# One written order for the change from the first to the second MLP, on all queues of one core

## The chip, the core and the metric

The kernel runs on one core of one Trainium2 chip. The metric is the device time of one execution in microseconds; before the change the median of three runs is 956.58 us (955.93 to 958.93). A core has five queues that work side by side: TensorE (PE, matmuls), VectorE (DVE), ScalarE (ACT), GpSimd (POOL) and SyncE (SP, which issues the transfers). Each of them takes its own instructions in one order, fixed when the program is built, and an instruction starts when the semaphores that it names have been reached.

## The reference

Sliding-window attention with a linear bias, and on its output two MLPs one after the other, both with a squared ReLU; the first has a scale s and an offset b. There are 2304 tokens (4 batches of 576), a model width of 512 and a hidden width of 2048, all in float32.

```python
attn_out = _attn_ref(q, k, v)                                # (4, 8, 576, 64)
x = attn_out.transpose(0, 2, 1, 3).reshape(2304, 512)
h = x @ moe_w_in;  r = np.maximum(h, 0.0)
x = (s * (r * r) + b) @ moe_w_out                            # first MLP
h = np.maximum(x @ moe2_w_in, 0.0)
out = (h * h @ moe2_w_out).astype(np.float32)                # second MLP
```

## The kernel before

Every float32 matmul of the MLPs is made of three matmuls on halves: a value is split into a rounded high part and the rest, and high times high, high times low and low times high are summed. The weights arrive as 64-bit words and are turned into such halves on the chip.

**Steps.** An MLP goes block by block over the tokens: four blocks of 512 tokens (the first MLP takes the first of them as two of 256) and a tail block of 256 that gathers the last 64 tokens of each batch. A block has 16 steps, one per 128 hidden columns. A step (`step_of`, L410) has a first layer of 12 matmuls into one PSUM bank (`first`, L414), a squaring (`square`, L428: ACT takes the ReLU out of the bank, DVE multiplies and frees the bank), a halving (`halves`, L437: ACT rounds to the high part, DVE subtracts), and a second layer of 12 matmuls (`one_second`, L451) that adds to the block's output banks. The first layers use two banks in turn, so the first layer of step n+2 waits until DVE has squared step n. All wide steps (512 tokens) share the one buffer `r_all`, so ACT's ReLU of a step waits for the halving of the step before. `mlp` (L474) writes the steps one after the other, with the second layers up to two steps behind the first.

**Names.** The change from the first to the second MLP has 37 steps, numbered 0 to 36: 16 narrow ones of the tail block of the first MLP (banks `ha`, 256 columns), five wide ones that are left of that MLP's last full block (`ha`, 512 columns; steps 4, 5, 10, 11, 12), and from step 21 on the 16 of block 0 of the second MLP (`hb`). `ga` and `gb` are the halved squares, `oa` and `ob` the output banks, `xoa` the outputs on their way to memory.

**What runs beside them.** In this stretch the second MLP's weights are loaded and converted, in 32 parts of 512 KB (4 groups of 8: four of `w_in`, four of `w_out`). A part is loaded into one of three staging buffers `st`, goes through a first stage (ACT, DVE), a second (ACT, DVE, two on POOL) and a third (ACT writes the high part `wih` or `woh`, DVE the low part `wil` or `wol`), which frees the buffer for the load of the third part after it. Group g of the second MLP takes the place of group g of the first, so the first of its third stages waits until the last step that reads the old group is done. Also in this stretch: the outputs of the two blocks of the first MLP are copied out of PSUM and written, the column sum for the offset is made (`pc`, `bcol`), and the second MLP's inputs `xib` are read back (`fetch`, L649), scaled by s with the offset added (four instructions on ACT per 256 tokens) and halved into `y` (`place`, L658: one DVE cast and one DVE subtraction per 256 tokens).

**What sets the order.** PE keeps the written order in the whole kernel. The attention stage is pinned: a table `START` (L39) lists its pieces, and the wrapper `InOrder` (L19) ties each instruction of ACT, DVE, POOL and SP to the one written before it, as long as `pinned` holds `True`. At L627 `pinned` is cleared. From there on a scheduler orders these four queues by its own estimates; `at(n, ...)` (L611) says before or after which step a piece is written, and `turns` (L693) hands out one conversion after the other, all three stages and the next load in one piece.

Of the kernel before, what the change touches and what calls it, by code (L numbers as in the profile page):

```python
# [50 lines left out]
"""  # L51

UNIT_ENGINES = """svvvvs vvvvss vvsvss vvvvsv vvvvvs vvvvss vvvvsv vsvssv vvvvss vvvvsv vvvvss vvvvss vvvvss vvsvsv vsvssv ssvsvv""".split()


@with_exitstack
def attention_mlp2_kernel(ctx, tc, first0, first1, qkv0, qkv1, qkvt, w_in1, w_out1, s_in, b_in, w_in2, w_out2, out):
# [76 lines left out]
    def act_copy(o, i):  # L134
        return scalar.activation(o, i, AF.Copy)
# [31 lines left out]
    def group_loads(g, wts, w_in, w_out, staging, steps):  # L167

        f0 = g * GF * P
        parts = [(w, k, n, st) for k, w, st in ((0, w_in, steps[0]), (2, w_out, steps[1])) for n in range(0, GF, st)]
        places = {}

        def load(i):
            if i == 0:
                wts.append({})
            w, k, n, step = parts[i]  # L180
            rows, n = slice(f0 + n * P, f0 + (n + step) * P), step
            if k == 0:
                w, rows, n = w[:, 2 * rows.start:2 * rows.stop], slice(None), NCC
            src = w[rows].rearrange("(a p) n -> p a n", p=P)
            t = places[i] = staging(i, f"st{g}{i}").rearrange("p a n -> p (a n)").rearrange("p (a n) -> p a n", a=n)

            with tc.issue_after(last_load[0]) if last_load else nullcontext():
                wdma.append(sync.dma_start(t, src).ins)

        def stages(i):  # L190
            def third():
                _, k, n, step = parts[i]
                if k not in wts[g]:
                    for j in (k, k + 1):
# [212 lines left out]
    def job(nm, x, wts, second, width, finish, o_tags, h_tags):  # L407
        return dict(nm=nm, x=x, wts=wts, second=second, width=width, finish=finish, o_tags=o_tags, h_tags=h_tags, po=[], n=0)
# [42 lines left out]
    def one_second():  # L451

        d, f, gh, lo, w, start, stop, _ = todo.pop(0)
        if start:
            d["po"] += [psum(d["o_tags"](), f"o{d['nm']}{i}") for i in range(d["width"] // P)]
        d["second"](d["po"], d["wts"][f // GF], f % GF, gh, start, stop, lo, w)
        if stop:
            d["finish"](d["po"])

    def second_layer(room):  # L460

# [54 lines left out]
    def finish1(nm, dram):  # L516
        def f(po):
            for t in range(2):
                xo = result(f"xo{nm}{t}")
                act_copy(xo, po[t])  # L520
                sync.dma_start(dram[:, 2 * t:2 * t + 2, :].rearrange("p a n -> p (a n)"), xo)
        return f

    def finish_pair(nm, i):
        def f(po):
            for o in range(NCC):
                xo = result(f"xo{nm}{o}", o > 1)
                (act_copy, vector.tensor_copy)[o % 2](xo, po[o])
                for u in range(2):
                    sync.dma_start(acc_dram[i + u][:, o, :], xo[:, u * BLK:(u + 1) * BLK])  # L530
        return f

    def finish2(nm, b):
        def f(po):
            for t in range(len(po)):
                ob = result(f"ob{nm}{t}", b == order[-1] and t > 0)
                if b == order[-1] and t == len(po) - 1:
                    for y, copy in enumerate((act_copy, vector.tensor_copy)):
                        cols = slice(y * BLK, (y + 1) * BLK)
                        copy(ob[:, cols], po[t][:, cols])  # L540
                        sync.dma_start(out[b * S + t * P:b * S + (t + 1) * P, cols], ob[:, cols])
                    continue
                (act_copy, vector.tensor_copy)[t % 2](ob, po[t])
                if b == "tail":
                    for r in range(P // TAIL):
                        row = (t * (P // TAIL) + r) * S + 2 * BLK
                        sync.dma_start(out[row:row + TAIL, :], ob[r * TAIL:(r + 1) * TAIL, :])
                else:
                    row = b * S + t * P
                    sync.dma_start(out[row:row + P, :], ob)  # L550
        return f

    blocks = [(b, u) for b in range(B) for u in range(2)] + ["tail"]
# [13 lines left out]
    def run(pieces):  # L567
        for p in pieces:
            p()
# [41 lines left out]
    def at(n, *pieces):  # L611
        slots.setdefault(n, []).extend(pieces)
# [36 lines left out]
    def fetch(nm, dram):  # L649

        xi = bp.tile([P, NCC, BLK], F32, tag="xi", name=f"xi{nm}")
        with tc.issue_after(last_load[0]) if last_load else nullcontext():
            sync.dma_start(xi, dram)
        for o in range(NCC):
            scalar.activation(xi[:, o, :], xi[:, o, :], AF.Identity, bias=bcol[:, o:o + 1], scale=s_sb)
        return xi

    def place(nm, xis):  # L658
        t = new_pair(nm)
        for u, xi in enumerate(xis):  # L660
            c = slice(u * BLK, (u + 1) * BLK)
            split(t[0][:, :, c], t[1][:, :, c], xi, vector.tensor_copy, dve_sub)
        return [y[:, :, :len(xis) * BLK] for y in t]
# [16 lines left out]
    def in_bp(i, nm):  # L680
        return bp.tile([P, 1, 2 * DM], I32, tag="st", name=nm, bufs=3)

    h_tags, y0, slots = tags("h", "t"), [], {}
    p6["h_tags"] = h_tags
    t8 = job(f"a{LAST}", lambda: x_tail[0], wts1, second_t, BLK, finish1(f"a{LAST}", acc_dram[LAST]), tags("s"), h_tags)
# [4 lines left out]
    groups = [group_loads(g, wts2, w_in2, w_out2, in_bp, (1, 1)) for g in range(NG)]  # L690
    loads, convs = [sum((x[k] for x in groups), []) for k in range(2)]
# [10 lines left out]
    cur = y0[2]  # L702
    last_load.clear()
    order = [0, 1, 2, "tail", 3]
    o_tags = tags("o", "o", "va", "vb", "s", "s")
    for b, after in zip(order, order[1:] + [None]):
        if b:
            last_load[:] = [wdma[-1]]
# [55 lines left out]
```

## Time and profile before

| | us |
|---|---|
| median of three runs | 956.58 (955.93 to 958.93) |
| the profiled execution, its own time | 956.87 |
| its span, first to last instruction | 955.1 |
| the 37 steps and one more: first matmul of step 0 to first matmul of block 1's second step | 464.88 to 645.11 |

The profile is of one execution. Its first part gives the busy time of each engine: PE is busy for 97% of the span. A busy share says little on a queue that waits for others in places, so the rows below are cut by stretches of time. "Idle before" in a row of the timeline is the time that the engine stood idle just before that instruction, and behind the arrow stands what ended it. Matmuls overlap: a row's duration (0.39 us at 512 columns) is longer than the distance to the next one's start. The clock is TensorE's granted clock as a share of the full 2.4 GHz; the other level is 1.2 GHz.

### The profile page before, as it was taken

The page shows a single profiled execution, that of the slowest core. Times are in us where ns is not written, and L with a number is a line of the kernel's source. Part 1 is how long each engine was busy: PE and PEld are TensorE (multiplying, and loading weights), DVE is VectorE, ACT ScalarE, POOL GpSimd, SP SyncE. Part 2 cuts the span into 40 slices and gives each one's busy share as a digit, 9 for nine tenths or more (in the row PEclk, how much of TensorE's full clock was granted, in tenths as well). Part 3 has the DMA queues.
Part 4 walks back from the last instruction along what each step waited for, and adds up shares of the span by engine and source line. Part 5 has one row for each costly group of instructions (what it writes and reads, how often), then busy time and mean ns, then how long its engine had stood idle before and what let it go on. Part 6 is the DMA issues. An engine that isn't in the chain of part 4 may idle for free.

```text
span 955.1 us, 13902 instructions
## 1 busy us (share of the span) xinstructions
PE 925.0 (97%) x5256; PEld 772.4 (81%) x5256; DVE 485.5 (51%) x1178; ACT 448.1 (47%) x1010; POOL 102.2 (11%) x164
## 2 busy tenths in 40 slices
PE   6899999999999999999999998999999999999998
PEld 4789998787777787777788886788888888998886
DVE  7988776445454455454377767444223222422222
ACT  7988775434444344454566666344223222422222
POOL 4333220000000000000124333100000000000000
PEclk7999999999999999999999999999999999999999
DMA  8642532201121111310334544012001000100001
GB/s 308 217 137 98 169 106 73 66 23 39 34 70 36 45 45 30 104 45 1 110 133 149 172 143 135 20 45 89 1 1 48 19 1 1 45 1 23 1 1 44
DMA packets 44227, 67.49 MB, mean 71 GB/s; under 512 B 6016, under 2 KB 27776, under 8 KB 44160
## 3 DMA queue, kind: packets, MB, share of 16 engines
q1 hardware_dynamic: 44160, 66.60, 21.6%
q8 instruction: 41, 0.67, 0.3%
q14 instruction: 26, 0.21, 0.1%
HBM read 57.15 MB, written 9.44 MB: 70 GB/s over the span
## 4 chain that ended last, share of the span: by engine, by line
PE 81%; DMA 6%; ACT 6%; DVE 5%; issue 1%; POOL 1%; SPq 0%; ACTq 0%; DVEq 0%
PE ha L29 18%; PE oa L29 17%; PE ob L29 16%; PE hb L29 16%; PE s L29 6%; DMA st<-w_out 3%; PE hbtail L29 2%; ACT st L29 2%; PE obtail L29 2%; DMA st<-w_in 2%; DVE st L29 2%; PE u L29 2%; PE s_t L29 1%; DVE wil L29 1%; PE u_t L29 1%
## 5 line engine op out<-in xcount | busy, mean ns | idle before, releaser
L29 DVE SCALAR_TENSOR_TENSOR r_all<-hb,r_all 128x512 f32<-128x512 f32 x64 | 44.1, 690 | 160.5 <-ACT r_all L29 160.2
L29 ACT ACTIVATE r_all<-hb 128x512 f32<-128x512 f32 x64 | 38.1, 595 | 171.1 <-PE hb L29 170.3
L29 POOL TENSOR_TENSOR st<-st 128x256 int32<-128x256 int32 x128 | 94.0, 761 | 210.8 <-DVE st L29 197.0
L29 DVE SCALAR_TENSOR_TENSOR r_all<-ha,r_all 128x256 f32<-128x256 f32 (+1 forms) x96 | 52.8, 553 | 102.1 <-ACT r_all L29 101.9
L29 ACT ACTIVATE st<-st 128x512 int32<-128x512 uint32 (+3 forms) x100 | 79.2, 813 | 29.6 <-DMA st<-w_in 12.0
L29 ACT ACTIVATE r_all<-ha 128x256 f32<-128x256 f32 (+1 forms) x96 | 46.2, 484 | 93.7 <-PE ha L29 92.2
L29 PE MATMUL oa<-ga,woh 128*128 128x256 f32 x384 | 73.1, 289 | 0.1
L29 PEld LDWEIGHTS oa<-ga,woh 128*128 128x128 f32 x384 | 60.7, 193 | 4.9 <-issue 3.5
L29 ACT ACTIVATE pr<-pr,nd 128x256 f32<-128x256 f32 (+1 forms) x102 | 48.0, 475 | 29.7 <-DVE nd L29 27.6
L29 DVE SCALAR_TENSOR_TENSOR st<-st 128x512 int32<-128x512 int32 (+1 forms) x50 | 44.1, 885 | 26.0 <-ACT st L29 22.9
L29 PE MATMUL oa<-ga,wol 128*128 128x256 f32 x192 | 54.4, 283 | 0.0
L29 PE MATMUL ha<-x0h,wih 128*128 128x256 f32 x128 | 37.3, 292 | 0.0
L29 PE MATMUL ha<-x0h,wil 128*128 128x256 f32 x128 | 36.4, 284 | 0.6 <-DVE wil L29 0.6
L29 PEld LDWEIGHTS oa<-ga,wol 128*128 128x128 f32 x192 | 36.9, 192 | 0.0
L29 PE MATMUL ha<-x0l,wih 128*128 128x256 f32 x128 | 36.2, 283 | 0.0
L29 PE MATMUL s<-raw 64*128 64x256 f32 (+1 forms) x224 | 32.5, 391 | 3.3 <-issue 1.5
L29 DVE CUSTOM_DVE_ANT_0 pr<-s,bases 128x256 f32<-128x256 f32 (+1 forms) x96 | 32.3, 386 | 3.5 <-PE s L29 3.4
L375 POOL MEMSET pr_t<- 128x64 f32 x16 | 2.4, 151 | 289.8 <-PE s L29 227.4
L29 DVE TENSOR_SCALAR st<-st 128x512 int32<-128x512 int32 (+1 forms) x50 | 28.2, 565 | 4.8 <-ACT st L29 3.4
L29 PE MATMUL hb<-y0h,wih 128*128 128x512 f32 x64 | 25.5, 398 | 5.2 <-DVE r_all L29 5.2
L29 PE MATMUL ha<-x3h,wih 128*128 128x512 f32 x64 | 27.1, 423 | 2.3 <-DVE r_all L29 2.3
L29 PEld LDWEIGHTS s<-raw 64*128 64x128 f32 x224 | 19.3, 191 | 9.7 <-issue 4.3
(685 smaller groups left out, 2599.0 us busy)
## 6 DMA issues: line engine op xcount, KB each, us to landing
st<-w_out SPq DMA_DIRECT2D x20, 512.0 KB, 4.4
st<-w_in SPq DMA_DIRECT2D x8, 1024.0 KB, 6.8
st<-w_in SPq DMA_DIRECT2D x16, 512.0 KB, 4.4
st<-w_out SPq DMA_DIRECT2D x6, 1024.0 KB, 8.1
raw<-qkv SPq DMA_DIRECT2D x36, 128.0 KB, 3.0
xib<-acc SPq DMA_DIRECT2D x9, 512.0 KB, 3.8
raw<-qkv SPq DMA_DIRECT2D x24, 160.0 KB, 3.0
out<-obb SPq DMA_DIRECT2D x15, 256.0 KB, 2.9
```

The lines of the kernel that those rows point to most:

```text
L29: ins = op(*args, **kw)
L375: nc.gpsimd.memset(pr[:, :Z], 0.0)
```

## The change

A second table, `HANDOVER`, lists the pieces of the 37 steps and of all that runs beside them in one order, and `pinned` is set for this stretch, so that ACT, DVE, POOL and SP keep that order instead of the scheduler's. The letters stand for: L, G, H, M the first layer, squaring, halving and second layer of a step (M always takes the oldest that is left); l, a, b, c with group and part the load and the three stages of a conversion; Y the load of 256 tokens of input; F and Q the scaling and halving of one half of them; E and W the copy out of PSUM and the write of an output; B the column sum. Inputs are handled in halves of two column groups, on ACT (s) or DVE (v) as two lists of letters say; the outputs' copies too. The input of block 1 is fetched, scaled and halved within the table. Output buffers `raw` are four instead of three, and the outputs no longer use the staging buffers, but for the last one of the kernel. Each of the pieces is written as before otherwise; PE has the same number of instructions, in a different order.

```diff
+HANDOVER = """
+    L0 G0 H0 L1 l00 l01 L2 G1 L3 a00 b00 B M c00 M0 l04 l02 a04 H1 a01 M1 G2 b01 G3 H2 L4 b04 H3 M2 M3 c01 L5 l05
+    a02 G4 b02 H4 c04 a05 l03 Y0 G5 c02 l06 a03 b05 H5 L6 G6 H6 c05 Y1 M4 l07 L7 a06 M5 G7 M6 b03 H7 b06 a07 F01
...
+EVICT_ENGINES, INPUT_ENGINES = "vsvs ss".split(), "vss svs svs svv vvs vvv vss vss".split()
...
-            return pools["bp"].tile([P, DM], F32, tag="raw", name=nm, bufs=3)
+            return pools["bp"].tile([P, DM], F32, tag="raw", name=nm, bufs=4)
...
+    def ways_out(nm, po, o, places, engine):
+        made = []
+        def evict():
+            made.append(result(f"xo{nm}{o}"))
+            copy_on[engine](made[0], po[o])
+        def write():
+            n = DM // len(places)
+            for u, (dram, c) in enumerate(places):
+                sync.dma_start(dram[:, c, :].rearrange("p a n -> p (a n)"), made[0][:, u * n:(u + 1) * n])
+        return evict, write
...
-                ob = result(f"ob{nm}{t}", b == order[-1] and t > 0)
+                ob = result(f"ob{nm}{t}", b == order[-1] and t > 2)
...
+    def scaled(xi, o, engine="s"):
+        if engine == "s":
             scalar.activation(xi[:, o, :], xi[:, o, :], AF.Identity, bias=bcol[:, o:o + 1], scale=s_sb)
+        else:
+            vector.tensor_scalar(xi[:, o, :], xi[:, o, :], s_sb, bcol[:, o:o + 1], ALU.mult, ALU.add)
...
+    def halve_input(u, h, engine):
+        if u // 2 not in ys:
+            ys[u // 2] = new_pair(f"y{u // 2}")
+        hi, lo = [y[:, 2 * h:2 * h + 2, u % 2 * BLK:(u % 2 + 1) * BLK] for y in ys[u // 2]]
+        split(hi, lo, xis[u][:, 2 * h:2 * h + 2, :], copy_on[engine], dve_sub)
...
-    run(loads[:3])
-    turns = [[*a, b] for a, b in zip(convs, loads[3:] + [lambda: None] * 3)]
-    for n in (4, 4, 5, 5, 6, 7, 8, 9, 10, 10, 11, 11, 12, 12, 13, 14, 15, 17, 18, 19):
-        at(2 * n, *turns.pop(0))
-    at(4, sum_column)
-    at(16, lambda: y0.append(fetch_y(0)))
-    at(24, lambda: y0.append(fetch_y(1)))
-    at(32, lambda: y0.append(place("y0", y0[:2])))
-    mlp(pieces_of(steps), slots)
...
+    pieces = pieces_of(steps + [(b0, f, 0, 2 * BLK) for f in range(NF)])
...
+    pinned.append(True)
+    run(table[x] for x in HANDOVER.split())
+    pinned.clear()
+    cur = ys[1]
+    for b, after in zip(order[1:], order[2:] + [None]):
...
-            at(26 if b == 0 else 2, lambda: nxt.append(load_y(after)))
-        for n in range(NF if b == 0 else 0):
-            if turns and n:
-                at(2 * n, *turns.pop(0))
+            at(2, lambda: nxt.append(load_y(after)))
```

**ACT at the start of the stretch.** Here `r_all<-ha_2` is the ReLU of step 2, on which PE waits for its bank; `xib` is the scaling of an input.

Before:

```order
L29 ACTIVATE r_all<-ha_1_4668 128x256
L29 ACTIVATE st_4648<-st_4648 128x512
L29 ACTIVATE st_4646<-st_4646 128x512
L29 ACTIVATE ga_1_4683<-r_all 128x256
L29 ACTIVATE st_4648<-st_4648 128x512
L29 ACTIVATE xib_4962<-xib_4962,bcol,s_sb 128x256 x4
L29 ACTIVATE xib_5164<-xib_5164,bcol,s_sb 128x256 x4
L29 ACTIVATE r_all<-ha_2_4704 128x256
L29 ACTIVATE wih_4760<-st_4644 128x4x128
```

Now:

```order
L29 ACTIVATE r_all<-ha_1_4662 128x256
L29 ACTIVATE st_4675<-st_4675 128x512 x2
L29 ACTIVATE wih_4731<-st_4675 128x4x128
L29 ACTIVATE st_4749<-st_4749 128x512
L29 ACTIVATE ga_1_4755<-r_all 128x256
L29 ACTIVATE st_4677<-st_4677 128x512
L29 ACTIVATE r_all<-ha_2_4679 128x256
```

The eight scalings stood between steps 1 and 2; now none stands there, and the first of them follows behind step 7.

**DVE at the halving of step 12.** `ga_12l` is the low half that step 12's second layer reads; `y0h` and `y0l` are the halves of block 0's input.

Before:

```order
L29 CAST y0h<-xib_4962 128x4x256
L29 CAST y0h<-xib_5164 128x4x256
L29 TENSOR_SCALAR st_5046<-st_5046 128x512
L29 SCALAR_TENSOR_TENSOR r_all<-ha_12_5170,r_all 128x512
L29 TENSOR_TENSOR y0l<-xib_4962,y0h 128x4x256
L29 TENSOR_SCALAR st_5099<-st_5099 128x512
L29 TENSOR_TENSOR y0l<-xib_5164,y0h 128x4x256
L29 SCALAR_TENSOR_TENSOR st_5109<-st_5109 128x512
L29 TENSOR_TENSOR ga_12l<-r_all,ga_12h 128x512
```

Now:

```order
L29 TENSOR_TENSOR ga_11l<-r_all,ga_11h 128x512
L29 TENSOR_SCALAR st_5040<-st_5040 128x512
L29 TENSOR_SCALAR st_5077<-st_5077 128x512
L29 SCALAR_TENSOR_TENSOR r_all<-ha_12_5136,r_all 128x512
L29 TENSOR_TENSOR ga_12l<-r_all,ga_12h 128x512
L29 TENSOR_TENSOR wil_5111<-st_5040,wih_5110 128x4x128
```

Four instructions that stood between the squaring and the halving of step 12 are gone from there; the halves of `y0` now come from step 15 on, in pieces.

**ACT at the halving of step 5.** `ga_5h` is its high half; `woh<-st` and `wih<-st` are third stages of conversions.

Before:

```order
L29 ACTIVATE r_all<-ha_5_4839 128x512
L29 ACTIVATE wih_4760<-st_4764 128x4x128
L29 ACTIVATE ga_5h<-r_all 128x512
L29 ACTIVATE woh_4876<-st_4774 128x512
L29 ACTIVATE r_all<-ha_6_4882 128x256
```

Now:

```order
L29 ACTIVATE woh_4856<-st_4749 128x512
L29 ACTIVATE st_4842<-st_4842 128x512
L29 ACTIVATE r_all<-ha_5_4829 128x512
L29 ACTIVATE wih_4731<-st_4751 128x4x128
L29 ACTIVATE st_4862<-st_4862 128x512
L29 ACTIVATE st_4842<-st_4842 128x512
L29 ACTIVATE ga_5h<-r_all 128x512
L29 ACTIVATE r_all<-ha_6_4882 128x256
```

The first stage of part 3 of group 0 (`st_4862`), which waits for a load, and a second stage now stand between the ReLU and the halving of step 5.

## Rows read from the trace of the kernel before

**Rows 1.** The page, busy us (share of the span) x instructions.

```profile
PE 925.0 (97%) x5256; PEld 772.4 (81%) x5256; DVE 485.5 (51%) x1178; ACT 448.1 (47%) x1010; POOL 102.2 (11%) x164
```

**Rows 2.** Windows: stretch, width, busy us (instructions) by engine, clock, DMA share, GB/s.

```profile
465.00:485.00 20.00, 18.00 (x116) 16.47 (x115) 10.86 (x22) 14.69 (x30) 4.46 (x6) 0.91 0.53 192
485.00:520.00 35.00, 34.72 (x211) 30.97 (x210) 25.55 (x43) 23.48 (x44) 13.61 (x18) 1.00 0.44 136
520.00:535.00 15.00, 11.84 (x66) 10.20 (x65) 12.98 (x21) 8.72 (x18) 6.85 (x8) 0.89 0.58 182
535.00:605.00 70.00, 64.83 (x346) 55.02 (x346) 48.18 (x78) 43.42 (x78) 25.43 (x33) 1.00 0.40 127
605.00:645.00 40.00, 40.00 (x178) 33.14 (x177) 15.72 (x23) 14.73 (x27) 0.00 (x0) 1.00 0.08 27
```

**Rows 3.** Waits of PE, 470 to 660 us: total us, times, longest.

```profile
PE hb L29 <- DVE r_all L29: 5.2, 4, 3.6
PE oa L29 <- DVE ga_12l L29: 3.2, 1, 3.2
PE ha L29 <- DVE r_all L29: 2.3, 2, 2.0
```

**Rows 4.** Timeline of PE: start, us, operation, [idle before <-what ended it].

```profile
464.88 0.28 PE L29 MATMUL ha<-xtailh,wih 128*128 128x256 f32 x1
...
467.75 0.40 PE L29 MATMUL oa<-ga_74h,woh 128*128 128x512 f32 x1
...
471.32 0.36 PE L29 MATMUL ha<-xtailh,wih 128*128 128x256 f32 x1
...
634.23 0.39 PE L29 MATMUL hb<-y0h,wih 128*128 128x512 f32 x1
...
636.95 0.39 PE L29 MATMUL ob<-woh,gb_13h 128*128 128x512 f32 x1
...
645.11 0.39 PE L29 MATMUL hb<-y1h,wih 128*128 128x512 f32 x1
```

**Rows 5.** Timeline of ACT at step 2.

```profile
473.04 4.05 ACT L29 ACTIVATE xib<-xib,bcol,s_sb 128x256 f32<-128x256 f32 x8 [0.86 <-DVE bcol L29]
477.00 0.36 ACT L29 ACTIVATE r_all<-ha 128x256 f32<-128x256 f32 x1
```

**Rows 6.** Timeline of DVE at the halving of step 12.

```profile
521.78 1.26 DVE L29 TENSOR_TENSOR y0l<-xib,y0h 128x1024 fp32r<-128x1024 f32 x1
...
523.72 1.21 DVE L29 TENSOR_TENSOR y0l<-xib,y0h 128x1024 fp32r<-128x1024 f32 x1
...
525.87 1.10 DVE L29 TENSOR_TENSOR ga_12l<-r_all,ga_12h 128x512 fp32r<-128x512 f32 x1
```

**Rows 7.** Timeline of ACT at step 25, the fifth of block 0.

```profile
579.18 1.22 ACT L29 ACTIVATE st<-st 128x512 int32<-128x512 uint32 x2 [2.10 <-DMA st<-w_in]
580.60 1.26 ACT L29 ACTIVATE st<-st 128x512 f32<-128x512 f32 x2 [0.20 <-DVE st L29]
581.74 0.58 ACT L29 ACTIVATE r_all<-hb 128x512 f32<-128x512 f32 x1
```

**Rows 8.** The staging tiles `st`, 460 to 620 us: durations min/median/max, and loads to landing.

```profile
L29 POOL TENSOR_TENSOR st<-st x64: 607/722/1596, 469.1 to 602.6; 128x256 int32<-128x256 int32 x64
L29 DVE TENSOR_TENSOR wol<-st,woh x16: 677/693/1097, 491.3 to 604.4; 128x512 fp32r<-128x512 f32 x16
DMA to landing us min/median/max: 3.3/4.4/5.6
```

**Rows 9.** Waits of ACT for loads, 464 to 605 us: total us, times, longest.

```profile
ACT st L29 <- DMA st<-w_in: 12.0, 10, 2.5
ACT st L29 <- DMA st<-w_out: 11.7, 13, 2.0
```

**Rows 10.** Groups by line and shape, 464 to 605 us: busy us, mean ns, idle before.

```profile
L29 ACT ACTIVATE st<-st 128x512 int32<-128x512 uint32 x32 | 21.6, 676 | 23.8 <-DMA st<-w_in 12.0 <-DMA st<-w_out 11.7
L29 DVE TENSOR_SCALAR st<-st 128x512 int32<-128x512 int32 x32 | 15.8, 492 | 3.0 <-ACT st L29 2.0
```

**Rows 11.** Timeline of DVE at the halving of step 5.

```profile
490.30 1.10 DVE L29 TENSOR_TENSOR ga_5l<-r_all,ga_5h 128x512 fp32r<-128x512 f32 x1
```

More of the change, by code (lines that the diff above doesn't have):

```diff
@@ L457, in one_second @@
         if stop:
-            d["finish"](d["po"])
+            for p in d["finish"](d["po"]):
+                p()
     def second_layer(room):
@@ L512, in result, with finish1, finish_pair @@
         if "bp" in pools:
-            return pools["bp"].tile([P, DM], F32, tag="raw", name=nm, bufs=3)
+            return pools["bp"].tile([P, DM], F32, tag="raw", name=nm, bufs=4)
         return ap.tile([P, DM], F32, tag="pr", name=nm, bufs=NPR)
-    def finish1(nm, dram):
+    copy_on = {"s": act_copy, "v": vector.tensor_copy}
+    def finish1(nm, dram, engines="ss"):
         def f(po):
[L518 to L521, printed above, removed]
+            evict, write = zip(*(ways_out(nm, po, t, [(dram, slice(2 * t, 2 * t + 2))], engines[t]) for t in range(2)))
+            return evict + write
         return f
-    def finish_pair(nm, i):
+    def finish_pair(nm, i, engines="svsv"):
         def f(po):
[L526 to L530, printed above, removed]
-        return f
+            return sum((ways_out(nm, po, o, [(acc_dram[i + u], slice(o, o + 1)) for u in range(2)], engines[o]) for o in range(NCC)), ())
+        return f
+    def ways_out(nm, po, o, places, engine):
[8 more added lines that the diff above has]
+        return evict, write
     def finish2(nm, b):
@@ L550, in f @@
                     sync.dma_start(out[row:row + P, :], ob)
+            return ()
         return f
@@ L653, in fetch @@
             sync.dma_start(xi, dram)
-        for o in range(NCC):
+        return xi
+    def scaled(xi, o, engine="s"):
+        if engine == "s":
             scalar.activation(xi[:, o, :], xi[:, o, :], AF.Identity, bias=bcol[:, o:o + 1], scale=s_sb)
-        return xi
+        else:
+            vector.tensor_scalar(xi[:, o, :], xi[:, o, :], s_sb, bcol[:, o:o + 1], ALU.mult, ALU.add)
     def place(nm, xis):
@@ L660, in place @@
         for u, xi in enumerate(xis):
+            for o in range(NCC):
+                scaled(xi, o)
             c = slice(u * BLK, (u + 1) * BLK)
@@ L681, in in_bp, with ends, f, load_input @@
         return bp.tile([P, 1, 2 * DM], I32, tag="st", name=nm, bufs=3)
-    h_tags, y0, slots = tags("h", "t"), [], {}
+    h_tags = tags("h", "t")
     p6["h_tags"] = h_tags
-    t8 = job(f"a{LAST}", lambda: x_tail[0], wts1, second_t, BLK, finish1(f"a{LAST}", acc_dram[LAST]), tags("s"), h_tags)
+    t8 = job(f"a{LAST}", lambda: x_tail[0], wts1, second_t, BLK, None, tags("s"), h_tags)
+    ways = {6: finish_pair("a6", 6, EVICT_ENGINES[0]), 8: finish1("a8", acc_dram[8], EVICT_ENGINES[1])}
+    out_of = {}
+    def ends(i):
+        def f(po):
+            out_of[i] = ways[i](po)
+            return ()
+        return f
+    p6["finish"], t8["finish"] = ends(6), ends(8)
+    order = [0, 1, 2, "tail", 3]
+    o_tags = tags("o", "o", "va", "vb", "s", "s")
+    ys, xis = {}, {}
+    def load_input(u):
+        xis[u] = fetch(f"b{u}", acc_dram[u])
+    def scale_input(u, h, engines):
+        for z in range(2):
+            scaled(xis[u], 2 * h + z, engines[z])
+    def halve_input(u, h, engine):
[3 more added lines that the diff above has]
+        split(hi, lo, xis[u][:, 2 * h:2 * h + 2, :], copy_on[engine], dve_sub)
+    b0 = job("b0", lambda: ys[0], wts2, second_n, 2 * BLK, finish2("b0", 0), o_tags, h_tags)
     steps = []
@@ L689, in attention_mlp2_kernel @@
         steps += [(p6, f, 0, 2 * BLK) for f in ((11, 12), (13, 14, 15), (), ())[g]]
-    groups = [group_loads(g, wts2, w_in2, w_out2, in_bp, (1, 1)) for g in range(NG)]
-    loads, convs = [sum((x[k] for x in groups), []) for k in range(2)]
-    run(loads[:3])
-    turns = [[*a, b] for a, b in zip(convs, loads[3:] + [lambda: None] * 3)]
-    for n in (4, 4, 5, 5, 6, 7, 8, 9, 10, 10, 11, 11, 12, 12, 13, 14, 15, 17, 18, 19):
-        at(2 * n, *turns.pop(0))
-    at(4, sum_column)
-    at(16, lambda: y0.append(fetch_y(0)))
-    at(24, lambda: y0.append(fetch_y(1)))
-    at(32, lambda: y0.append(place("y0", y0[:2])))
-    mlp(pieces_of(steps), slots)
[L702 to L708, printed above, removed]
+    pieces = pieces_of(steps + [(b0, f, 0, 2 * BLK) for f in range(NF)])
+    table = {"M": one_second, "B": sum_column}
+    for g in range(NG):
+        for i, (l, c) in enumerate(zip(*group_loads(g, wts2, w_in2, w_out2, in_bp, (1, 1)))):
+            table.update({f"{x}{g}{i}": p for x, p in zip("labc", [l] + c)})
+    for n, piece in enumerate(pieces):
+        table.update({f"{x}{n}": p for x, p in zip("LGHM", piece)})
+    for i, n in ((6, NCC), (8, 2)):
+        for o in range(n):
+            x, y = (2 * o, 2 * o + 1) if i == 6 else (o, o + 2)
+            table.update({f"E{i}{o}": lambda i=i, x=x: out_of[i][x](), f"W{i}{o}": lambda i=i, y=y: out_of[i][y]()})
+    for u in range(4):
+        table[f"Y{u}"] = lambda u=u: load_input(u)
+        for h in range(2):
+            e = INPUT_ENGINES[2 * u + h]
+            table[f"F{u}{h}"] = lambda u=u, h=h, e=e: scale_input(u, h, e[:2])
+            table[f"Q{u}{h}"] = lambda u=u, h=h, e=e: halve_input(u, h, e[2])
+    pinned.append(True)
[3 more added lines that the diff above has]
+    for b, after in zip(order[1:], order[2:] + [None]):
+        last_load[:] = [wdma[-1]]
         nxt, slots = [], {}
```

10 lines of the change are left out of this document (added).

## The prediction

> **What bounds the kernel now.** I read the page's busy shares first: PE is busy for 925.0 of 955.1 us, DVE for 485.5, ACT for 448.1 [rows 1]. PE sets the time, and a change can give back only what PE loses. Its work is the same after the change (as many matmuls, in another order), so the question is how much PE loses in the 37 steps, and how much of that a new order can remove.
>
> Cut by stretches, PE lacks 2.00 us in 465 to 485, 0.28 in 485 to 520, 3.16 in 520 to 535 and 5.17 in 535 to 605, together 10.6 us; from 605 on it is full [rows 2]. The waits put nearly all of it down to DVE: 5.2 us on the squaring in block 0, 3.2 us on the low half of step 12, 2.3 us on the squaring in the narrow and wide steps of the first MLP [rows 3]. The clock is lost twice beside that: 0.91 over the 20 us around the wait at step 4 and 0.89 over the 15 us around the one at step 12, so in both places the lower level, 1.2 GHz, was granted for part of the time [rows 2]; 20 x 0.09 + 15 x 0.11 = 3.5 us. The 5.17 us of 535 to 605 cost no clock (1.00).
>
> What PE would need without any loss: a narrow layer takes (467.75 - 464.88) / 2 = 1.435 us, a wide one 636.95 - 634.23 = 2.72 us, and the second layer of the last step before together with the column sum 471.32 - 467.75 = 3.57 us [rows 4]. From 464.88 to the start of block 1's second step there are 32 narrow layers (45.9 us), that pair (3.57) and 42 wide layers (114.2): 163.7 us. The ten wide layers of the first MLP in this stretch run a little slower (some 0.03 us each), so 164.0. The trace takes 645.11 - 464.88 = 180.2 us [rows 4]. **The loss is 16.2 us**: 10.6 idle, 3.5 of clock, and the remaining 2 at the restarts, where the first matmul after a wait is slow and the idle time counts only from the modelled end of the last one.
>
> **The three large waits, and what the change does to each.** The first: ACT scales both inputs of block 0 in one run of eight, 473.04 to 477.09, and only then takes the ReLU of step 2, at 477.00 [rows 5]; PE waits 2.0 us for the bank and then runs at a lower clock. In the new order the eight scalings are gone from there, and between the ReLUs of steps 1 and 2 stand five stages of conversions and one halving. Counted from the end of step 1's first layer these take 6 x 0.6 = 3.6 us on ACT (two stages in 1.22 us [rows 7]), 2 to 3 us in which the third stage waits for DVE and POOL, and the squaring, some 7.5 us. PE has 9.3 us of other layers between the same two points (two narrow first layers, the column sum, one wide and two narrow second layers), so this wait goes. The second: between the squaring and the halving of step 12 stand two subtractions for `y0` (1.26 and 1.21 us) and two instructions of conversions, so that `ga_12l` comes at 525.87 [rows 6]; now it follows the squaring at once, and PE asks for it one wide second and three narrow first layers, 7.0 us, after step 12's first layer, some 4 us after it is ready. The third: in block 0's fifth step ACT does two first stages, waiting 2.10 us for a load, and two second stages before the ReLU, which comes at 581.74 [rows 7]; in the new order one first stage stands between the ReLUs of the fourth and the fifth step, and PE asks for the bank only three wide layers (8.2 us) after the fifth step's first layer. These three are 2.0 + 3.2 + 3.6 us of idle time and all of the clock. The remaining 1.9 us are four waits of under 0.8 us on the squaring; the new order puts the ReLU in front of the conversions there too.
>
> **What the moved work needs.** The conversions are all still there. Over 465 to 605 DVE is busy for 10.9 + 25.6 + 13.0 + 48.2 = 97.6 us and ACT for 90.3 [rows 2], of 140; the new order spreads them, and the input of block 1 as well, over 156 us (steps 0 to 36 at 164.0 less three wide layers), up to the last steps of block 0. Ten of the sixteen scalings of blocks 0 and 1 go to DVE. Such a scaling on DVE is in no row; on ACT one takes 0.5 us [rows 5], and a DVE instruction with constants over twice the columns takes 0.49 [rows 10]. Between 0.2 and 0.6 us each, I take the 0.49, 5 us in all; with the last steps of block 0 and block 1's input, which the old trace has in 605 to 645 (15.7 us on DVE [rows 2]), DVE stands at 118 of 156 us. If it were full there, each further us would be one of PE; it isn't by some 38.
>
> The staging buffers set the pace of the conversions: a load takes 4.4 us to land (3.3 to 5.6) [rows 8], the three stages some 4 to 5 us more, so three buffers allow one part in about 3 us, or 97 us for 32 parts. There are 150 for them. Only at the start are the margins small, because the third stages of group 0 wait for steps 0 to 3.
>
> **Where the new order can make PE wait.** I went along the new order from one first layer to the next, adding durations behind whatever ends last. Two places have no margin.
>
> Step 5's halving: the third stage of `w_out`'s first part waits until step 3's second layer is done, as the old group is read until then. Counted from there: third stage on ACT and DVE 1.35 us, the load into the buffer that this frees 4.4, its first stage on ACT 0.68, the second stage of another part 0.6, the high half of step 5 0.6, and behind it on DVE `ga_5l` 0.69: 8.3 us. PE in that time does one wide and one narrow first layer, a wide second and a narrow first: 2.72 + 1.44 + 2.72 + 1.44 = 8.3. With a load of 5.6 us it is 1.2 us late, with one of 3.3 early by as much. In the trace before, `ga_5l` took 1.10 us [rows 11] instead of some 0.69, as do some other DVE subtractions (677 to 1097 ns), while POOL's adds take 607 to 1596 [rows 8]; I take 0.4 for that and 0.2 for the hand-overs, so 0.6 us of waiting.
>
> The Trainium skill speaks against placing a halving there: its page "SBUF — State Buffer", section "Who interferes with whom", has a DVE instruction with two SBUF inputs and a GpSimd one that reads SBUF lock each other out for a whole instruction. The slowed rows agree that DVE loses time, but with 0.41 us, less than POOL's median of 0.72. By the page's rule the wait at step 5 would be 0.9 us and the time 0.3 us longer.
>
> Step 10's halving is the same case: the load behind the third stage of `w_in`'s last part, then its first stage, then `ga_10h`. Counted from the end of step 9's first layer: a halving, a scaling and the ReLU on ACT 1.5, the third stage 1.35, the load 4.4, the first stage 0.68, `ga_10h` 0.6, `ga_10l` 0.69, together 9.2 us; PE has three narrow and two wide layers, 9.8. That is a margin of 0.6 us, and 0.6 late if the load takes 5.6. Step 11 has as much. I take 0.5 us for the two together.
>
> From step 16 on every margin that I find is over 1 us, and growing: ACT and DVE go ahead of PE there, since nothing but the ReLU of the next step holds them.
>
> **Edits at nothing.** Outputs copied by another engine, in four own buffers: six copies, each hidden by the 38 us that DVE has, due only when block 0 or block 1 takes the bank. SP's order: all writes but the last wait for a copy made over 5 us earlier, so no load of weights is held by one. The kernel's last outputs in other buffers: the same copies, at most one load's wait of 4 us if a buffer were still being read, which it is not one block later. Block 1's input within the table: done before step 34, needed after step 36.
>
> **Sum.** 956.87 of the profiled execution - 16.2 + 0.6 + 0.5 = 941.6; the median of the runs is 0.3 lower than that execution. I say 941.8.
>
> **The rivals.**
> *New waits with a lower clock.* The old places are gone, but two others stall as long as the first and the second did: 2.0 + 1.8 + 0.3 and 3.2 + 1.7 + 0.3 = 9.3 us. For it: two places without margin, and an order of 32 chained loads in which a late one holds the next. Against: PE waits 0.28 to 0.76 us in the old trace four times without losing any clock. 956.9 - 16.2 + 9.3 = 950.0.
> *The waits only move.* The order was not the cause, the loads were: the same 10.6 us of idle time return elsewhere, with clock and restarts. For it: ACT waited 23.7 us for loads [rows 9]. Against: at the two waits with clock loss no load stands in the chain [rows 5, 6]. 956.9.
> *Slower: a load in front of everything.* In the fixed order each first stage on ACT stands ahead of ReLUs, and a late load holds them all. ACT waited 23 times, 1.03 us on average [rows 9], mostly with nothing to do behind it; if PE pays each, 956.9 - 16.2 + 23.7 = 964.4. It is slower than before from 16.2 / 32 = 0.5 us per part. Against: from step 21 on most loads land before ACT comes to their stage.
>
> **Chances.** The forecast 0.71, its own range 940.4 to 944.5 (all loads early, or step 5, 10 and 11 at the late end with one short loss of clock); two new waits 0.17; moved 0.06; slower 0.06. The range of 8 in 10 is 940.0 to 951.0. A measurement of this kernel can tell 0.3% (2.9 us) from no change: faster by that 0.88, same 0.06, slower 0.06.
>
> **What would show it.** Right: PE idle under 2 us between 464 and 630, a clock of 1.00 there, block 1's second step starting at 629 to 631, the ReLU of step 2 by 475. The steps on the margins are right if what waits is PE for `ga_5l` or `ga_10l`, by less than 1.5 us. Wrong: PE waits of over 2 us anywhere, ACT waiting for loads ahead of a ReLU that PE needs, or a clock under 0.97 in a stretch of 15 us.

## The result and the profile after

The changed kernel takes 941.46 us (median of four runs, 940.88 to 941.92), the kernel before 956.79, measured beside it: a ratio of 0.9836, with a 95% interval of 0.9819 to 0.9853. Forecast: 941.8. The profiled execution took 941.92 us, its span is 940.1.

The page's busy shares, which answer to [rows 1]:

```profile
PE 918.9 (98%) x5256; PEld 769.7 (82%) x5256; DVE 485.0 (52%) x1190; ACT 445.5 (47%) x1006; POOL 96.7 (10%) x164
```

DVE and ACT are busy for about as long as before; PE does the same 5256 matmuls in 6 us less of busy time and fills 98% of a shorter span. The same five stretches as in [rows 2] (busy us of PE, PEld, DVE, ACT and POOL with their instructions, then the clock, the DMA share and GB/s):

```profile
465.00:485.00 20.00, 20.00 (x139) 18.66 (x138) 12.36 (x23) 10.94 (x22) 5.93 (x8) 1.00 0.38 128
485.00:520.00 35.00, 35.00 (x212) 31.32 (x211) 23.32 (x43) 22.07 (x43) 9.17 (x14) 1.00 0.43 141
520.00:535.00 15.00, 15.00 (x116) 14.51 (x116) 11.13 (x23) 10.38 (x24) 3.93 (x6) 1.00 0.47 153
535.00:605.00 70.00, 70.00 (x342) 59.32 (x341) 51.24 (x87) 45.30 (x81) 19.73 (x28) 1.00 0.40 127
605.00:645.00 40.00, 40.00 (x178) 33.11 (x177) 23.13 (x34) 21.15 (x37) 6.08 (x8) 1.00 0.39 125
```

PE is full in each of them, and the clock is 1.00 in all. The view of PE's waits over these 37 steps has no line any more, where [rows 3] had three. The two ends of the stretch on PE, as in [rows 4] (first matmul of step 0, first of block 1's second step):

```profile
466.05 0.28 PE L29 MATMUL ha<-xtailh,wih 128*128 128x256 f32 x1
...
630.19 0.39 PE L29 MATMUL hb<-y1h,wih 128*128 128x512 f32 x1
```

630.19 - 466.05 = 164.14 us, against 180.23 before. This length is the measure for all that follows. Between its two marks PE has the same layers in all these kernels, and the length does not depend on when step 0 begins, which is anywhere from 464.81 to 466.05 in the profiled executions. ACT at step 2, answering to [rows 5], and DVE at step 12, answering to [rows 6]:

```profile
474.84 0.68 ACT L29 ACTIVATE st<-st 128x512 int32<-128x512 uint32 x1
475.42 0.37 ACT L29 ACTIVATE r_all<-ha 128x256 f32<-128x256 f32 x1
```

```profile
515.41 0.69 DVE L29 SCALAR_TENSOR_TENSOR r_all<-ha,r_all 128x512 f32<-128x512 f32 x1 [1.19 <-ACT r_all L29]
516.80 0.69 DVE L29 TENSOR_TENSOR ga_12l<-r_all,ga_12h 128x512 fp32r<-128x512 f32 x1 [0.70 <-ACT ga_12h L29]
```

Step 2's ReLU now follows a first stage, not eight scalings, and begins 9.4 us after step 0 where it was 12.1 (475.42 - 466.05, 477.00 - 464.88; "by 475" had been said, from a step 0 that began 1.17 us earlier); `ga_12l` is ready at 517.49, and PE begins step 12's second layer at 521.62. ACT's waits for loads in the stretch, as in [rows 9] (total us, times, longest):

```profile
ACT st L29 <- DMA st<-w_out: 4.7, 3, 2.7
ACT st L29 <- DMA st<-w_in: 2.6, 3, 1.1
```

Six waits of 7.3 us in all, instead of 23 of 23.7. At step 5, the first place said to be without margin, ACT, then DVE, then POOL:

```profile
484.06 0.68 ACT L29 ACTIVATE woh<-st 128x512 fp32r<-128x512 f32 x1 [0.82 <-PE oa L29]
...
489.16 1.24 ACT L29 ACTIVATE st<-st 128x512 int32<-128x512 uint32 x2 [1.13 <-DMA st<-w_in]
490.28 0.63 ACT L29 ACTIVATE ga_5h<-r_all 128x512 fp32r<-128x512 f32 x1
```

```profile
490.94 0.69 DVE L29 TENSOR_TENSOR ga_5l<-r_all,ga_5h 128x512 fp32r<-128x512 f32 x1
```

```profile
490.97 1.70 POOL L29 TENSOR_TENSOR st<-st 128x256 int32<-128x256 int32 x2 [6.36 <-DVE st L29]
```

The chain is the predicted one: third stage behind PE, load, first stage, `ga_5h`, `ga_5l`. It ends at 491.63, and PE asks for `ga_5l` at 492.5: 0.9 us early.

### The profile page after: what moved, and what is told of

It reads as the page before. It is cut to its first block, busy times and chain, and to the rows that moved or that the text cites. A ratio compares the mean times of both kernels' runs of the same rounds, so it can differ in the third digit from the quotient of the medians.

```text
span 940.1 us, 13895 instructions
## 1 busy us (share of the span) xinstructions
PE 918.9 (98%) x5256; PEld 769.7 (82%) x5256; DVE 485.0 (52%) x1190; ACT 445.5 (47%) x1006; POOL 96.7 (10%) x164
## 4 chain that ended last, share of the span: by engine, by line
PE 92%; ACT 4%; DVE 1%; DMA 1%; issue 0%; SPq 0%; POOL 0%; ACTq 0%
PE oa L29 21%; PE ha L29 21%; PE hb L29 19%; PE ob L29 19%; PE s L29 6%; PE hbtail L29 2%; PE obtail L29 2%; PE u L29 2%; ACT st L29 1%; PE s_t L29 1%; DMA st<-w_out 1%; PE u_t L29 1%; ACT f_3woh L29 0%; ACT f_0wih L29 0%; ACT pr L29 0%
## 5 line engine op out<-in xcount | busy, mean ns | idle before, releaser
L29 POOL TENSOR_TENSOR st<-st 128x256 int32<-128x256 int32 x128 | 88.5, 720 | 234.7 <-DVE st L29 221.2
L29 ACT ACTIVATE st<-st 128x512 int32<-128x512 uint32 (+3 forms) x100 | 79.8, 815 | 20.0 <-DVE st L29 10.7
L29 ACT ACTIVATE pt<-s 128x512 f32<-128x512 f32 (+1 forms) x43 | 21.4, 538 | 11.5 <-PE s L29 11.3
```

The lines of the kernel that those rows point to most:

```text
L29: ins = op(*args, **kw)
```

## The experiments

All are variants of the changed kernel, but for one of the kernel before. "Stretch" is the length defined above, from the profile of each: 164.1 us without any loss.

### Which queue has to keep the order

The written order alone, with the four queues left to the scheduler:

```diff
-    pinned.append(True)
     run(table[x] for x in HANDOVER.split())
```

> The pieces are written in the new order, but ACT, DVE, POOL and SP are not tied to it: the scheduler may reorder them, and PE alone keeps the new order. If the kept order on the four queues is what removes the waits (my theory), the scheduler again puts the conversions or the scalings ahead of a ReLU or a halving in some places: between 3 and 12 us of the 16 come back, 945 to 953 us. Rival: the order in which things are written, with PE's new order, is enough; then 941 to 943 us and no wait of PE over 1 us.

Measured: 958.59 us, ratio to before 1.0019 [1.001, 1.0029], stretch 181.1. All of the gain is gone, more than the 3 to 12 us that I had expected. The largest wait, DVE and then PE:

```profile
525.54 1.97 DVE L29 TENSOR_SCALAR xib<-xib,s_sb,bcol 128x256 f32<-128x256 f32 x4
527.43 0.74 DVE L29 SCALAR_TENSOR_TENSOR r_all<-ha,r_all 128x256 f32<-128x256 f32 x2
```

```profile
527.90 0.58 PE L29 MATMUL ha<-xtailh,wih 128*128 128x256 f32 x1 [4.64 <-DVE r_all L29]
```

The scheduler puts four scalings of an input, which PE does not need for a long time yet, ahead of the squarings that it needs now. They are 1.97 of the 4.64 us; before them three subtractions of an input (1.88 us) already stood ahead of `ga_12l`, as in the kernel before, and the ReLUs waited for that. PE's new order and the new choice of engines are in this kernel too; without the kept order they give nothing. Then one queue at a time, by what is tied to the table (`scalar` is ACT, `vector` DVE):

```diff
-    pinned.append(True)
+    scalar.on = [True]
     run(table[x] for x in HANDOVER.split())
-    pinned.clear()
+    scalar.on = pinned
```

> The new written order, PE's too, but only ACT is tied to it in these 37 steps; DVE, POOL and SP are left to the scheduler (with all four left to it the time was 958.6 us: DVE had four scalings of the next input, 1.97 us, ahead of a squaring, and two halvings of an input ahead of that of step 12). My theory: both queues can put work ahead of what PE waits for, so ACT alone gives back a part only: 944 to 953 us. Rival: ACT's order decides, since it holds the stages that wait for loads and DVE follows ACT's results; then 941 to 943 us.

Measured: 944.15 us, 0.9864 [0.9848, 0.9881], stretch 167.4. The waits of PE:

```profile
PE ha L29 <- DVE r_all L29: 1.0, 1, 1.0
PE oa L29 <- ACT ga L29: 0.8, 1, 0.8
PE oa L29 <- DVE ga L29: 0.6, 1, 0.6
```

ACT's order alone gives 13 of the 16 us (a stretch of 167.4 instead of 180.2). The first wait is DVE's doing: it stood 1.98 us waiting for an input's load and scaled that, ahead of the squaring. The same edit with `vector` in place of `scalar`:

> The new written order with DVE alone tied to it; ACT, POOL and SP are left to the scheduler. My theory: ACT is the queue on which stages that wait for loads or for POOL stand ahead of ReLUs, so tying DVE alone gives back less than tying ACT alone (which gave 13 of 16): 946 to 956 us, with PE waits of over 1.5 us on squarings whose ReLU came late on ACT. Rival: either queue is enough, since the two exchange results at every stage and so hold each other to the order: 941 to 944.5 us.

Measured: 959.57 us, 1.0028 [1.0019, 1.0038], stretch 182.0: nothing is won, and the time lies above even the 946 to 956 of my theory. ACT's waits for loads in this kernel:

```profile
ACT st L29 <- DMA st<-w_out: 18.5, 14, 3.2
ACT st L29 <- DMA st<-w_in: 15.8, 13, 2.7
```

34.3 us in 27 waits. With ACT free it was 23.6 us in 23 waits in the kernel without any tie, 23.7 in the kernel before; with ACT tied it is 6.1 in the run above and 7.3 in the changed kernel. So what ACT's order does is visible: a first stage stands far enough behind its load that the load has mostly landed. DVE, held to its order alone, passes on what ACT does late. At one place in block 0 it stands still for 3.85 us before a third stage of ACT's, and the squaring for which PE waits stands behind that:

```profile
572.09 0.69 DVE L29 TENSOR_TENSOR wol<-st,woh 128x512 fp32r<-128x512 f32 x1 [3.85 <-ACT woh L29]
572.70 0.68 DVE L29 SCALAR_TENSOR_TENSOR r_all<-hb,r_all 128x512 f32<-128x512 f32 x1
```

```profile
573.43 0.50 PE L29 MATMUL hb<-y0h,wih 128*128 128x512 f32 x1 [1.75 <-DVE r_all L29]
```

On ACT that third stage stood behind another one that waited 1.39 us for POOL and a first stage that waited 0.85 us for its load. And both, `scalar.on = vector.on = [True]`, with POOL and SP free:

> The new written order with ACT and DVE tied to it; POOL and SP are left to the scheduler (which brings the input loads two places earlier on SP). ACT alone tied gave 944.2 us. My theory: the rest is lost on DVE's queue (halvings and squarings behind other work), and the orders of POOL and SP cost nothing, as the prediction had it: 941 to 942.5 us, no wait of PE over 0.5 us. Rival: SP's order matters, since a load that an input load is put ahead of comes late: 943 to 945 us.

Measured: 941.22 us, 0.9833 [0.9818, 0.9849], stretch 164.1, no wait of PE. With these two kept, the order of POOL and SP costs and gives nothing.

### The places of the old waits

The eight scalings put back on ACT ahead of step 2's ReLU, the two inputs loaded early:

```diff
-    ... l04 l02 a04 H1 a01 M1 G2 ...
+    ... l04 Y0 Y1 l02 a04 H1 a01 M1 F00 F01 F10 F11 G2 ...
-INPUT_ENGINES = "vss svs svs svv ..."
+INPUT_ENGINES = "sss sss sss ssv ..."
```

> The table as it is, but the first two inputs are loaded early and their eight scalings stand on ACT in one run between the halving of step 1 and the ReLU of step 2, as in the kernel before. My theory: the first of the three waits returns and nothing else; PE waits 1.5 to 3 us for the bank at step 4, the clock falls behind it (another 1.8 us), 944.5 to 947 us. Rival: with all else in order the ReLU still comes in time, no wait over 0.5 us, 941 to 942.5 us.

Measured: 944.32 us, 0.9868 [0.9852, 0.9884], stretch 167.7. On ACT, on PE, and the stretch of the windows:

```profile
475.13 4.03 ACT L29 ACTIVATE xib<-xib,bcol,s_sb 128x256 f32<-128x256 f32 x8
479.07 0.36 ACT L29 ACTIVATE r_all<-ha 128x256 f32<-128x256 f32 x1
```

```profile
479.94 0.50 PE L29 MATMUL ha<-x3h,wih 128*128 128x512 f32 x1 [1.76 <-DVE r_all L29]
```

```profile
465.00:485.00 20.00, 18.24 (x115) 16.47 (x114) 10.04 (x19) 12.44 (x26) 4.29 (x6) 0.91 0.46 158
```

The stretch is 3.6 us longer: 1.76 of waiting and 20 x 0.09 = 1.8 of clock. That is the first wait of the kernel before, in place and size, and at nearly its price (4.1). The profiled execution, 945.22 us, is one of the longer of the four (942.49 to 945.52); between the medians the price is some 3 us.

The same question from the other side: the kernel before, with block 0's input scaled and halved only behind step 15. The scalings move from `fetch` into `place`, and:

```diff
-    at(32, lambda: y0.append(place("y0", y0[:2])))
+    def place_y0():
+        with tc.issue_after(last_g[0]), tc.issue_after(last_g[1]):
+            y0.append(place("y0", y0[:2]))
+    at(32, place_y0)
```

> The kernel before, with one edit: the scaling and the halving of block 0's input are tied behind the halving of step 15, on ACT and on DVE; everything else is left to the scheduler. My theory of the three waits says that the first (scalings ahead of the ReLU of step 2, 2.0 + 1.8 + 0.3 us) and the second (halving of the input ahead of step 12's, 3.2 + 1.7 + 0.3 us) go, and the third stays: 956.8 - 9.3 = 947.5, between 946 and 949.5 us. Rival: without an order for all queues the waits only move, since the conversions take the free places; 952 to 957 us.

Measured: 956.90 us, 0.9996 [0.9985, 1.0006], stretch 180.1. My theory fell: both places are cleared (the first wait is gone, `ga_12l` costs 0.55 instead of 3.16 us), and not a microsecond is won. A new wait, on ACT and on PE:

```profile
530.19 1.21 ACT L29 ACTIVATE st<-st 128x512 int32<-128x512 uint32 x2 [1.06 <-DMA st<-w_in]
531.29 0.66 ACT L29 ACTIVATE woh<-st 128x512 fp32r<-128x512 f32 x1
531.86 0.65 ACT L29 ACTIVATE st<-st 128x512 f32<-128x512 f32 x1
532.41 0.64 ACT L29 ACTIVATE r_all<-ha 128x256 f32<-128x256 f32 x2
```

```profile
533.82 0.58 PE L29 MATMUL ha<-xtailh,wih 128*128 128x256 f32 x1 [3.73 <-DVE r_all L29]
```

Conversions have taken the free place: two first stages that wait for a load, a third and a second stage stand ahead of two ReLUs. PE's idle time over the stretch is again 10.7 us, as in the kernel before (10.6). One of its waits, 1.33 us at 542.52, comes behind the moved scalings and halvings themselves (ACT 534.12 to 538.73), so not all of it is the conversions' doing.

The halving of block 0's input put between the squaring and the halving of step 12, where it stood before, in the kept order:

```diff
-    ... M11 L13 H12 c11 c14 ...
+    ... M11 L13 Q00 Q01 Q10 Q11 H12 c11 c14 ...
```

(F00 comes ahead for it, from behind step 15 to behind step 10.)

> The new order, but the whole halving of block 0's input (three casts on ACT, one cast and four subtractions on DVE, some 3.2 us on DVE) stands between the squaring and the halving of step 12, about where the old kernel had it and lost 5 us. In the changed kernel ga_12l is ready at 517.5 and PE asks for it at 521.6 us, 4.1 us later. My theory: what makes the place costly is not the place but how soon PE asks; 3.2 us fit into the 4.1, so no wait, 941 to 942.5 us. Rival: the step's halving is late anyway (the input's casts wait for each other on two engines) and the wait with its lower clock returns: 944 to 947 us.

Measured: 942.69 us, 0.9849 [0.9832, 0.9865], stretch 165.9. Counted from step 0, `ga_12l` is 2.7 us later than in the changed kernel and still in time; what is late is the next step, ACT and PE:

```profile
519.67 0.39 ACT L29 ACTIVATE r_all<-ha 128x256 f32<-128x256 f32 x1 [1.50 <-DVE ga_12l L29]
```

```profile
521.17 0.38 PE L29 MATMUL ha<-xtailh,wih 128*128 128x256 f32 x1 [1.25 <-DVE r_all L29]
```

The ReLU of step 13 waits for the halving, because they share `r_all`, and PE for its bank. Neither theory had that wait. The place costs 1.7 us here; in the kernel before the prediction put it at 5.2.

And the margin at step 5, with the input loads ahead of the weight load in question:

```diff
-    ... c04 a05 l03 Y0 G5 ... H6 c05 Y1 M4 ...
+    ... c04 a05 Y0 Y1 l03 G5 ... H6 c05 M4 ...
```

> The new order, but SP issues the two input loads (512 KB each) ahead of the load of w_in's last part of group 0 (the one whose first stage stands before the halving of step 5 on ACT), instead of behind it. In the changed kernel ga_5l is ready at 491.6 us, PE asks at 492.5: 0.9 us of margin. My theory (the margin is that of the load): the load lands 1.5 to 3.5 us later, PE waits 0.6 to 2.6 us for ga_5h or ga_5l, with a lower clock behind it if the wait is over 1.5 us; 942 to 946 us. Rival: the transfers overlap and the load lands within 0.9 us of before; 941 to 942 us, no wait.

Measured: 941.05 us, 0.9831 [0.9814, 0.9847], stretch 164.1, no wait. The edit did not delay what it was to delay: the input loads wait for no buffer, went out at 480.05 and landed within 5.2 us, while the weight load waited for its buffer until 484.53, as late after step 0 as in the changed kernel (19.4 us). So the run says nothing on the margin.

### PE's own order

PE's layers in the order of the kernel before, the other queues in the table's. A first variant also moved the column sum B ahead of G0, and with it its small DVE instruction:

```diff
-    L0 G0 H0 L1 l00 l01 L2 G1 L3 a00 b00 B M c00 M0 ... L4 ... M2 M3 ... L5 ...
+    L0 L1 M B G0 L2 H0 l00 l01 G1 L3 M0 a00 b00 c00 ... L4 M1 ... M2 L5 ... M3 ...
```

> The four other queues keep the table's order, but PE's layers stand in the order of the kernel before: second layers follow one or two layers earlier behind their first layer than in the table. If the order of the other queues does the work (my theory), PE loses little: in the narrow steps the second layer is asked for after one first layer less, so the margins at steps 5 and 10 shrink by 1.4 us each and 0 to 3 us are lost, 941.5 to 944.5 us. Rival: PE's own new order, with its longer distance between first and second layer, is what removes the waits; then waits at steps 4, 5, 10 to 12 return with the lower clock behind them, 947 us or more.

Measured: 952.37 us, 0.9956 [0.9943, 0.9968], stretch 175.1. DVE's rows show why:

```profile
472.05 0.22 DVE L29 TENSOR_SCALAR bcol<-pc,b_sb 128x4 f32<-128x4 f32 x1 [7.03 <-PE pc L29]
472.19 0.41 DVE L29 SCALAR_TENSOR_TENSOR r_all<-ha,r_all 128x256 f32<-128x256 f32 x1
```

An instruction of 0.22 us stands ahead of step 0's squaring and waits for PE; DVE stands still for 7 us and all stages behind it are late. With B behind b00, as in the table:

> As the earlier run with PE's old order of layers, but the column sum's small DVE instruction keeps its place in the table (behind two stages of conversions); there it had stood ahead of the squaring of step 0. Only the first and second layers of PE are in the old order; ACT, DVE, POOL and SP keep the table's. My theory: the earlier 11 us came mostly from that misplaced instruction; with the table's order on the other queues PE loses only where a second layer now comes one layer earlier (steps 4 to 5 and 10 to 12), 1 to 5 us, 942.5 to 946.5. Rival: the table of the other queues and PE's order only work as a pair, since the first second layers of PE now delay steps 2 and 3 and with them all conversions of group 0 by some 3 us; 948 to 953 us.

Measured: 947.76 us, 0.9897 [0.9882, 0.9913], stretch 170.8. The place of the column sum and its one small instruction was 4.3 us of the stretch, and 6.7 are still lost by PE's order, between my theory and the rival. The waits of PE:

```profile
PE ha L29 <- DVE r_all L29: 3.6, 3, 1.3
PE oa L29 <- ACT ga_5h L29: 1.4, 1, 1.4
PE oa L29 <- DVE ga_5l L29: 0.2, 1, 0.2
```

Step 5 shows how the two orders hang together. The third stage of `w_out`'s first part waits for step 3's second layer, which the table has PE do ahead of step 5's first layer, and the old order behind it:

```profile
487.50 0.67 ACT L29 ACTIVATE woh<-st 128x512 fp32r<-128x512 f32 x1 [3.90 <-PE oa L29]
...
492.74 1.23 ACT L29 ACTIVATE st<-st 128x512 int32<-128x512 uint32 x2 [2.96 <-DMA st<-w_in]
493.87 0.61 ACT L29 ACTIVATE ga_5h<-r_all 128x512 fp32r<-128x512 f32 x1
```

ACT waits 3.90 us instead of 0.82, the next load goes out 4.3 us later, counted from step 0, and `ga_5h` is 1.4 us late.

### Engines and staging buffers

Scalings all on ACT, casts and copies as in the kernel before:

```diff
-EVICT_ENGINES, INPUT_ENGINES = "vsvs ss".split(), "vss svs svs svv vvs vvv vss vss".split()
+EVICT_ENGINES, INPUT_ENGINES = "svsv ss".split(), "ssv ssv ssv ssv ssv ssv ssv ssv".split()
```

> The new order kept on all queues, but every scaling of an input is on ACT and every cast on DVE, and the outputs are copied by ACT and DVE as in the kernel before: ACT gets ten scalings of some 0.55 us more, DVE those less. My theory: with DVE busy for about 121 and ACT for about 111 of 156 us neither engine is the bound, and the scalings stand where there is room; 941 to 942.5 us. Rival: longer runs of scalings on ACT use up margins ahead of ReLUs around steps 7 to 16; one or two waits of 0.5 to 1.5 us, 942.5 to 945 us.

Measured: 941.85 us, 0.9838 [0.9822, 0.9855], stretch 165.3. Beside the run with ACT and DVE tied on the same chip (941.22) the difference is not to be told from none in the times. The stretch is 1.2 us longer in the profile; PE's waits in it are two, of 0.22 and 0.14 us, and the clock is 1.00.

Two staging buffers instead of three, and in the table each load moved behind the third stage of the part two places earlier, with what had stood ahead of that. The buffers' line alone is shown here:

```diff
-        return bp.tile([P, 1, 2 * DM], I32, tag="st", name=nm, bufs=3)
+        return bp.tile([P, 1, 2 * DM], I32, tag="st", name=nm, bufs=2)
```

> The new order with two staging buffers for the weight parts instead of three; each load stands behind the third stage of the part two places earlier, and whatever had stood ahead of that is moved behind it. The prediction's pace: a buffer is taken for a load of 3.5 to 4.4 us and stages of 4 to 5, so two buffers allow a part in about 4.3 us, 137 us for 32, against 97 with three; and ACT comes to a first stage before its load has landed. My theory: the pace binds, ACT waits 1.5 to 3 us for most of the 32 loads with ReLUs behind them, and PE pays a third to two thirds of it: 955 to 985 us. Rival: the loads still fit into the 156 us and the margins absorb the waits; 941 to 946 us.

Measured: 1015.62 us, 1.0611 [1.059, 1.0631], stretch 239.6. ACT's waits for loads, 464 to 720 us:

```profile
ACT st L29 <- DMA st<-w_out: 56.0, 13, 6.1
ACT st L29 <- DMA st<-w_in: 30.3, 11, 4.8
```

86 us in 24 waits; the time is far above both ranges. PE idles 47 of the 240 us, and at a clock of 0.90 loses 24 more. A load still lands in 3.6 us (median, as in the changed kernel); it is late because it goes out late. So (load + stages) / buffers, which gives 137 us for two, is not the pace of this kept order: here a buffer comes free when its third stage's turn comes. The rest of the table was laid out for three buffers; what one laid out for two would lose is not shown.

## Why the prediction was right, and where it was not

- **PE's loss of 16.2 us, all from the order of the queues: right.** 180.23 - 164.14 = 16.1, and the sum's 164.0 us of dense work is met to 0.1. Left to the scheduler, the same pieces lose all of it again; with ACT and DVE held to the table nothing is lost.
- **The three waits, each with its own cause: right as a description, wrong as a cause that can be taken away singly.** The first was rebuilt in the kept order at nearly the price given (3.6 us). But in the old kernel the first two could be removed without any gain: the free queues filled the places, mostly with conversions that wait for loads, and even the third changed (2.07 us with a loss of clock instead of 3.60 without). "The waits only move", a rival at 0.06 for the whole change, is what happens to a part of it. The gain is that of an order, ACT's first of all and DVE's for the rest, not a sum over three places. Why the scheduler takes first stages so early is not shown by any run. Nor was the written order of the kernel before run with its queues tied, so how much any kept order would give, and how much needs this table, stays open.
- **The 0.6 us at step 5 and 0.5 at steps 10 and 11: wrong, none came.** At step 5 the load took 3.67 us from issue to first stage where 4.4 was taken, and `ga_5l` 0.69, not the 1.10 of [rows 11]: it began 0.03 us ahead of POOL's two adds, and these took longer instead, 1.70 us where such a pair takes 1.2 undisturbed. The Trainium skill's page "SBUF — State Buffer", section "Who interferes with whom", has the two lock each other out. These rows agree, with POOL as the one that waited, some 0.5 us.
- **The sum: added up wrong, and near the result by luck.** 956.87 - 16.2 + 0.6 + 0.5 is 941.8 for the profiled execution, not 941.6, and 0.3 less is 941.5 for the median, not 941.8. The 1.1 us of waits did not come, yet the profiled execution took 941.92 us, since its step 0 began 1.17 us later (466.05 against 464.88). The changed stretch has no part in that: one and the same matmul of the first MLP (`oa<-ga_32h,woh`) is 1.16 us late already at 175.03 (173.87 before). The stretch alone is the fair measure: 164.1 us, where 164.0 + 1.1 was forecast. Among the arguments one number was misread: the four short waits that cost no clock begin at 0.16 us, not at 0.28.
- **The margin of about 4 us at step 12: right** (4.1), but it is not the whole margin of the place: the next step's ReLU has less.
- **Engine loads: no bound, as said, and less than forecast.** DVE is busy for 108.4 of the 156 us from 466 to 622, where 118 was taken; a scaling on DVE takes 0.41 us, where 0.49 was taken. Which engine takes the scalings hardly matters.
- **SP's order: nothing, as said, and POOL's as well.** The outputs' own buffers were taken back in no run; that they cost nothing is shown only by the stretch without waits.
- **The staging pace: not borne out.** With two buffers its formula leaves 19 us to spare, and the kernel lost 75. That three suffice is shown by the profile alone.
- **PE's order** entered the prediction as the time at which PE asks. It is worth more than that: PE also releases the old weights, and with them the loads.

## What to carry to other kernels

Where a free order makes an engine wait in several places, removing single places may give nothing, as here: tie first the queue on which instructions wait for loads, and see what is left. In a kept order every queue's order, the bound engine's included, is part of one schedule: an instruction of 0.22 us at the wrong place, waiting for PE, cost 4.3 us. Measure the length of the changed stretch between two marks on the bound engine beside the whole time: what happens outside the stretch then passes neither for a gain nor for a hit.

## What the runs showed of the hardware

In the changed kernel's stretch, DVE subtractions with two inputs in SBUF (128x512) took 0.68 to 0.70 us in all 49 cases without POOL work beside them, and 0.69 to 1.09, 0.91 on average, in the ten that lay beside it for their whole length (to 0.03 us); the five wide squarings wholly beside POOL work, with one input in PSUM, took 0.69 throughout.

The length of a wait alone does not tell what it does to PE's clock. Waits of 1.25 to 1.40 us left it at 1.00 in the second run with PE's old order, and so did one of 1.75 in block 0 of the run with DVE alone tied; one of 1.76 at step 4 brought it to 0.91 over 20 us. At one and the same step of block 0, the kernel before and that kernel with its input held:

```profile
583.55 0.50 PE L29 MATMUL hb<-y0h,wih 128*128 128x512 f32 x1 [3.60 <-DVE r_all L29]
```

```profile
583.54 0.50 PE L29 MATMUL hb<-y0h,wih 128*128 128x512 f32 x1 [2.07 <-DVE r_all L29]
```

From 580 to 600 us the clock is 1.00 with the longer wait and 0.91 with the shorter one, so part of that stretch ran at the lower level, 1.2 GHz. The limit of 1.5 us that one expectation above assumed is not borne out.
